# Moving the first weight loads, four kinds of VectorE work and one activation load in a fused linear-attention and mixer kernel

## The chip, the cores and the metric

The kernel runs on one core of a Trainium2 chip. The metric is the device time of one execution in microseconds (us); the median of three runs before the change is 294.98. In the text PE is TensorE, DVE is VectorE, ACT is ScalarE, POOL is GpSimd and SP is SyncE. A "slot" is a place in the kernel's own list of work, explained below.

## What is computed

Inputs are q, k and v (8 batches, 8 heads, 576 positions, head size 64) and the mixer's U, V, w_ch1 and w_ch2. All are 32-bit floats; the kernel works in bf16 with 32-bit sums.

```python
def phi(x, c, s):
    r = np.maximum(x, 0.0)
    return np.concatenate([r * c, r * s], axis=-1)
q_p = phi(q, cos_w, sin_w)
k_p = phi(k, cos_w, sin_w)
kv = np.einsum('bhsf,bhsd->bhfd', k_p, v)
z = np.sum(k_p, axis=2)
num = np.einsum('bhsf,bhfd->bhsd', q_p, kv)
den = np.einsum('bhsf,bhf->bhs', q_p, z)[..., None] + 1e-06
x = num / den                      # heads side by side: (8, 576, 512)
u = x + (x.transpose(0, 2, 1) @ U @ V).transpose(0, 2, 1)
out = u + np.maximum(u @ w_ch1, 0.0) @ w_ch2
```

The weights w_ch1 (512 x 2048) and w_ch2 (2048 x 512) are the same for all batches.

## The kernel before

**Tiles.** A batch's 576 positions are four full tiles of 128 (c = 0 to 3) and a tail of 64 (c = 4); the tails of two batches share a tile. For each batch, `q_prep` and `k_prep` make the features (one cosine and one sine operation for each tile, line 304 on DVE, line 302 on ACT), the q features are transposed (`qtr_unit` on PE for batches 0 and 1, by DMA later), `kv_unit` sums k features times v, and `x_unit` or `x_two` multiply q features by kv and divide by the denominator: a reciprocal on DVE (lines 408 and 409) and the norms, which multiply by it. `x_two` (line 1253) works on a tile in two halves of four heads; its norms are one DVE operation for each half (line 1280), and for batch 1 four ACT operations for each half (line 1274). `A_unit` multiplies by U, its result is cast to `A_sb`, `u_mm` (line 471) multiplies by V, and `u_add` adds x. Then comes the hidden layer, `g1_main` (line 572) with a ReLU on ACT (line 581), and the product with w_ch2: `g2_part` (line 744) for the first two batches, `half_part` (line 873) later. `half_part` multiplies in seven partial products instead of eight; for that it needs sums of hidden tiles (`hid_sum`, line 818) and sums of quarters of w_ch2 in `w2_s[0]` to `w2_s[3]`, made once by `w2_sum` (line 789), each in two halves of 128x1024. It uses them from slot 90 on.

**Order.** The order of work is written out by hand, and every engine runs its instructions strictly in the order in which the program issues them. The start (batch 0, lines 1176 to 1230) is straight code. From there a list `slots` holds the PE work and `todo` what is issued behind each slot: slots 0 to 15 are the hidden layer of batch 0, 16 to 31 products of batch 0, 32 to 47 the hidden layer of batch 1, 48 to 51 the first tails, 52 to 71 further products, 72 to 87 the hidden layer of batch 2, and from 88 on hidden layer and products alternate. `attention_plan` puts the attention of batches 2 to 7 between them: batch 2's `kv_unit` stand at slots 46 and 48, batch 3's at 64 and 66, its `x_two` at 69 and 73. In slot 1 PE comes to the transposes of batch 1's q tail (line 361), behind eight matmuls of `g_half` (line 589) and the four that complete the first two tiles of the hidden layer.

**Transfers.** SP issues the loads of q, k and v in a fixed order; each batch's load is an "odd" and an "even" DMA of 64 rows. One of them waits at SP until the staging buffer (`qst`, `kst`, `vst`) has been read by the features of the batch before, and what is behind it waits too. POOL issues the weights' loads, which cast to bf16 on the way: `load_v0` (heads 0 to 3 of batch 0's v, straight to bf16 in `v0`, an odd and an even half), the four column blocks of w_ch1 (`w1_load`, line 117) and the four blocks of w_ch2 (line 123). POOL also casts U and V (`cast_u`, `cast_v`). Two small copies to `mark` on POOL hold back what follows: the first until batch 0's k has landed (line 1214, ahead of w_ch1), the second until batch 1's k has landed (line 1225, ahead of w_ch2). `gate` (line 1238) is the same on SP: a tiny DMA into `mark2` that must wait for its source. In `first_chain` (line 1113) batch 0 goes from k features to the hidden layer; its last instructions on ACT and DVE are followed directly by batch 1's `q_prep`.

Of the kernel before, what the change touches and what calls it, by code (L numbers as in the profile page):

```python
# [17 lines left out]
def kernel(  # L18
# [11 lines left out]
    nc = tc.nc  # L30
# [12 lines left out]
    TS = 64  # L43
# [13 lines left out]
    class Banks:  # L57
# [21 lines left out]
    qst, kst, vst = [  # L79
        pool.tile([P, H, 5, D], FP32, tag=name, bufs=1, name=name)  # L80
        for name in ("qst", "kst", "vst")
    ]
# [10 lines left out]
    def load_odd(dst, src, b, h0=0, h1=H):  # L93
        nc.sync.dma_start(
            out=dst[1:P:2, h0:h1, 0:4].rearrange("m h c d -> m h (c d)"),
            in_=nines(src, b)[:, h0:h1, 5 * D : 9 * D],
        )
# [17 lines left out]
    def w1_load(n):  # L115
        cs = slice(n * 512, n * 512 + 512)
        nc.gpsimd.dma_start(
            out=w1_bf[:, :, cs], in_=moe_w_ch1.rearrange("(d p) n -> p d n", p=P)[:, :, cs]
        )
# [35 lines left out]
    def load_v0():  # L155
        nc.gpsimd.dma_start(
            out=v0[1:P:2, :, 0:4].rearrange("m h c d -> m h (c d)"),
            in_=nines(v, 0)[:, 0:4, 5 * D : 9 * D],
        )
        nc.gpsimd.dma_start(  # L160
            out=v0[0:P:2].rearrange("m h c d -> m h (c d)"),
            in_=nines(v, 0)[:, 0:4, 0 : 5 * D],
        )
# [92 lines left out]
    def cast_u():  # L256
        cast(G_, U_bf[:, 0:4, :], stU[:, 0:4, :])
        for i in range(2):
            cast(G_, U_bf[tail(i), 4 + i, :], stU[tail(i), 4, :])
# [75 lines left out]
    def kv_unit(b, hg, tag, bufs, eng=None, n=E):  # L335
        if b not in kv_sb:
            kv_sb[b] = pool.tile([P, H, E], BF16, tag="kv", bufs=2, name="kv")
        acc = ps.tile([P, 4, n], FP32, tag=tag, bufs=bufs, name="kv_ps")
        vx = v_ext
        for i in range(4):  # L340
            h = hg * 4 + i
            for c in range(5):
                nc.tensor.matmul(  # L343
                    out=acc[:, i, :],
                    lhsT=k_of(b, c, h),
                    rhs=v_tl[:, h, 0:n] if c == 4 and b < 2
                    else vx[:, c if c < 4 else 4 + b % 2, h, 0:n],
                    start=(c == 0),
                    stop=(c == 4),
                )  # L350
        cast(eng or V_, kv_sb[b][:, hg * 4 : hg * 4 + 4, 0:n], acc)
# [431 lines left out]
    def w2_sum(n, half):  # L783

        a, b = (
            (W2[1], W2[0]), (W2[3], w2_s[0]), (W2[3], W2[1]), (W2[2], w2_s[1])
        )[n]
        js = slice(4 * half, 4 * half + 4)
        V_.tensor_tensor(
            out=w2_s[n][:, js], in0=a[:, js], in1=b[:, js], op=ALU.subtract  # L790
        )
# [171 lines left out]
    def spare(at):  # L963
        if at < 72:
            return ("o", 2) if 32 <= at < 52 else ("g", 3)
        return ("o", 2) if at < 88 else ("s", 1)
# [14 lines left out]
    def attention_plan(b):  # L981

        plan = []
        if b < 4:
            w, f_at, q_eng, k_eng, qtr, lo = PLAN[b]
        else:
            w, q_at, k_at, qtr, lo = PLAN[b]

        def put(at, f, *a, tag=False):
            if tag:  # L990
                a = a + spare(w + at)
            plan.append((w + at, lambda: f(b, *a)))

        for n, c in enumerate(QORD):
            if b > 3:
                put(q_at[0] + q_at[1] * n, q_prep, c, q_at[2:])
                put(k_at[0] + k_at[1] * n, k_prep, c, k_at[2:])
                put(k_at[0] + (3 * n) // 2, v_prep, 0, H, (c,), (G_,))
                continue
            if b == 3:  # L1000
                q_eng, k_eng = V_ if n == 3 else A_, A_ if n < 3 else None
                put((-12, -11, -10, -7, -3)[n], q_prep, c, (q_eng, q_eng))
                put(n - 9 if n < 3 else -5, k_prep, c, (A_, k_eng))
                if n > 2:
                    put(2 * n - 12, k_prep, c, (None, V_))
                put(-4 if n > 2 else -6, v_prep, 0, H, (c,), (A_ if n > 2 else G_,))
                continue
            put(f_at + ((n - 1) % 5 if b == 2 else n), q_prep, c, (q_eng, q_eng))
            put(f_at + 6 + n, k_prep, c, (k_eng, k_eng))
            on_v = b == 2 and n > 2  # L1010
            put(
                -5 if on_v else f_at + 3 + (3 * n) // 2,
                v_prep, 0, H, (c,), (V_ if on_v else G_,),
            )
        for n, (c0, c1) in enumerate(((4, 5), (0, 2), (2, 4))):
            at = qtr[n] if b > 4 else 1 if b == 3 and n == 2 else qtr + 2 * n
            put(at, qtr_dma, c0, c1)
        plan.append((w, lambda: kv_unit(b, 0, *spare(w), A_ if b > 3 else V_)))
        plan.append((w + 2, lambda: kv_unit(b, 1, *spare(w + 2), A_ if b > 3 else V_)))
        for n, c in enumerate(ORD):  # L1020
            if b > 3:
                put(4 + 2 * n, x_unit, c, "X", 1)
            elif n % 2:
                put(9 if (b, n) == (3, 3) else 4 + (3 * n) // 2, x_two, c, tag=True)
            else:
                put(4 + (3 * n) // 2, x_unit, c, "X", 1)
        a_at = 15 - b if b < 4 else 14
        put(a_at, A_unit, tag=True)
        odd = b % 2 == 1


        def two(at):
            return [T1, ("s", 1)] if at >= 88 else [spare(at)] * 2

        plan.append((w + a_at + 2, lambda: u_mm(b, *two(w + a_at + 2))))
        for j in range(4):
            put(a_at + 2 + j + (2 if b > 4 and j > 1 else 0), u_add, j)
        put(a_at + 3, utr_dma, 0, 2)
        put(a_at + (7 if b > 4 else 5), utr_dma, 2, 4)
        if odd:  # L1040
            plan.append(
                (w + a_at + 9, lambda: u_tail(b // 2, *two(w + a_at + 9)))
            )
            put(a_at + 10, utr_dma, 4, 5)
        for at, t in zip(lo, loads(b + 1) if lo else ()):
            plan.append((w + at, t))
        return plan
# [141 lines left out]
    keep_warm(4, "X", 1)  # L1189
    cast_v()  # L1190
    load_v0()
    cast_u()
    spread_v()
    z_all = ps.tile([P, 2, 512], FP32, tag="X", bufs=1, name="z_ps")
# [16 lines left out]
    kv0_mm(kv_lo, range(3, 5))  # L1211
    keep_warm(1, *G3)

    G_.tensor_copy(out=mark, in_=kst[0:TS, 7, 4, 0:1])
    for n in range(4):
        w1_load(n)
    first_chain(0)
    load_odd(qst, q, 1)
    load_even(qst, q, 1)
    load_odd(kst, k, 1)  # L1220
# [32 lines left out]
    def x_two(b, c, *hi):  # L1253
        x_alloc(b)
        rows = slice(0, P) if c < 4 else tail(b)
        if not hi and not side:
            side["g"] = ps.tile([P, 512], FP32, tag="g", bufs=3, name="side")
        lo = ps.tile([P, 512], FP32, tag="T", bufs=1, name="x2_ps")
        up = ps.tile([P, 512], FP32, tag=hi[0], bufs=hi[1], name="x2_ps") if hi else side["g"]
        accs = [  # L1260
            t[:, 0 : 4 * E].rearrange("p (i e) -> p i e", e=E) for t in (lo, up)
        ]
        for h in range(H):
            nc.tensor.matmul(
                out=accs[h // 4][:, h % 4, :], lhsT=qT_of(b, c, h), rhs=kv_sb[b][:, h, :],
                start=(h % 4 == 0), stop=(h % 4 == 3),
            )
        rec = pool.tile([P, 2, 4], FP32, tag="rec", bufs=2, name="rec")
        n = P if c < 4 else TS
        for g, acc in enumerate(accs):  # L1270
            recip(rec[rows, g, :], acc[rows, :, D])
            if b == 1:
                for i in range(4):
                    nc.scalar.activation(
                        out=x_of(b, c)[:, (4 * g + i) * D : (4 * g + i + 1) * D],
                        in_=acc[:, i, 0:D], func=AF.Copy, bias=0.0,
                        scale=rec[:, g, i : i + 1],
                    )
                continue
            nc.vector.tensor_tensor(  # L1280
                out=x_of(b, c, rows)[:, g * 256 : g * 256 + 256].rearrange(
                    "p (i d) -> p i d", d=D
                ),
                in0=acc[rows, :, 0:D],
                in1=rec[rows, g, :].unsqueeze(2).to_broadcast([n, 4, D]),
                op=ALU.mult,
            )
# [18 lines left out]
    def put(at, thunk):  # L1306
        todo.setdefault(at, []).append(thunk)
# [92 lines left out]
    for i, go in enumerate(groups):  # L1400
        slots.append(go)
        if i < 14:
            n, i7 = halfs[i]
# [24 lines left out]
    put(at - 2, lambda: tail_store(nc.sync, 3, o_last(1), slice(0, 512)))  # L1428
    put(at - 1, lambda: tail_store(A_, 2, o_last(0), slice(256, 512)))
    for n in range(8):  # L1430
        put((56, 58, 60, 62, 66, 67, 69, 70)[n], lambda n=n: w2_sum(n // 2, n % 2))
    for j, ts_ in beside.items():
        todo[j] = list(ts_) + todo.get(j, [])

# [49 lines left out]
```

## Time and profile before

| what | value |
|---|---|
| median of 3 runs (lowest, highest) | 294.98 us (294.69, 295.87) |
| the profiled execution | 296.47 us |
| its span, first to last instruction | 294.7 us |
| mean granted TensorE clock | 1.00 |
| share of the chain that ended last | PE 89%, DVE 5%, issue 2%, DMA 2%, ACT 1% |
| HBM read, written | 36.86 MB, 9.44 MB |

How to read the views: a timeline line gives start and length in us, the engine, the line of the kernel, the operation, what it writes and reads, and in brackets how long its engine was idle before it and which engine's work ended that. "x4" means that four alike were merged. "SPq" is SP's queue; a DMA's line there is its issue, not its transfer. The chain of waits follows back from the last instruction what each step waited for. In the DMA view q1 is the queue that SP feeds and q0 the one that POOL feeds; both run on the same 16 DMA engines; its lines give packets, MB, and the packets' own time as a share of the window (over 100% in sum where packets overlap).

### The profile page before, as it was taken

What the parts mean: (1) busy time and instruction counts of PE and PEld (TensorE: products, weight loads), DVE (VectorE), ACT (ScalarE), POOL (GpSimd) and SP (SyncE); (2) the same over time, 40 slices, a digit from 0 to 9 for tenths busy, and PEclk for the clock granted to TensorE, in tenths of its full rate; (3) what the DMA queues carried; (4) which work ended last, traced back from release to release, by engine and by line L of the source; (5) the groups of instructions that cost most, each with busy time, mean ns of one, the idle gap of its engine ahead of it and who ended that gap; (6) DMA issues with size and microseconds to landing.
All of it is one profiled execution on the core that took longest, in us unless ns stands there. A gap on an engine that the chain in (4) does not pass through costs nothing.

```text
span 294.7 us, 7180 instructions
## 1 busy us (share of the span) xinstructions
PE 285.6 (97%) x2884; PEld 194.3 (66%) x2922; DVE 210.1 (71%) x503; ACT 157.6 (53%) x305; POOL 50.5 (17%) x89
## 2 busy tenths in 40 slices
PE   8999999999989999999999999999999999999995
PEld 6685554446645445676757666766877668889884
DVE  4988745694698978837736794678747788785863
ACT  2956853175890357568735865378752334446310
POOL 8800400012020001310500311031200100000340
PEclk9999999999999999999999999999999999999999
DMA  6999999999996999999499919992900141101013
GB/s 215 337 252 254 255 195 186 204 317 252 325 145 92 300 260 243 225 304 308 122 231 283 266 38 242 237 342 56 221 31 2 73 89 73 72 2 71 2 72 145
DMA packets 90709, 54.07 MB, mean 183 GB/s; under 512 B 58420, under 2 KB 87380, under 8 KB 90676
## 3 DMA queue, kind: packets, MB, share of 16 engines
q1 hardware_dynamic: 84116, 43.85, 59.7%
q0 software_dynamic: 6416, 9.63, 14.6%
q8 instruction: 23, 0.38, 0.5%
q10 hardware_dynamic: 144, 0.13, 0.1%
q14 instruction: 10, 0.08, 0.1%
HBM read 36.86 MB, written 9.44 MB: 157 GB/s over the span
## 4 chain that ended last, share of the span: by engine, by line
PE 89%; DVE 5%; issue 2%; DMA 2%; ACT 1%; DVEq 0%; ACTq 0%
PE g_ps L572 32%; PE h_ps L873 26%; PE o_ps L744 8%; PE gt_ps L706 5%; PE c_ps L666 4%; PE kv_ps L343 3%; PE x_ps L418 3%; DMA qst<-in_q_dram 2%; PE h_ps L744 1%; PE a_ps L441 1%; DVE k_p L304 1%; PE t_ps L373 1%; PE va_ps L471 1%; PE t_ps L361 1%; DVE x_bf L428 1%
## 5 line engine op out<-in xcount | busy, mean ns | idle before, releaser
L581 ACT ACTIVATE hid<-g_ps 128x512 bf16<-128x512 f32 x112 | 66.6, 597 | 85.0 <-PE g_ps L572 84.7
L572 PE MATMUL g_ps<-uT,w_bf 128*128 128x512 bf16 x414 | 105.1, 379 | 1.3
L572 PEld LDWEIGHTS <-w_bf 128*128 128x128 bf16 x440 | 41.4, 98 | 36.8
L873 PEld LDWEIGHTS <-hid 128*128 128x128 bf16 x480 | 45.4, 98 | 9.6
L873 PE MATMUL h_ps<-w_bf,hid 128*128 128x256 bf16 x288 | 37.0, 273 | 0.0
L831 DVE TENSOR_TENSOR o_sb<-u_bf,h_ps 128x256 f32<-128x256 bf16 x44 | 18.3, 416 | 18.2 <-PE h_ps L873 17.9
L744 PE MATMUL o_ps<-w_bf,hid 128*128 128x512 bf16 x122 | 29.4, 379 | 0.4 <-issue 0.2
L131 POOL CAST v_ext<-vst 128x512 bf16<-128x512 f32 (+1 forms) x26 | 17.9, 716 | 52.2 <-DMA vst<-in_v_dram 42.5
L873 PE MATMUL h_ps<-w_s,S 128*128 128x256 bf16 x208 | 26.5, 273 | 0.0
L873 PE MATMUL h_ps<-w_s,hid 128*128 128x256 bf16 x192 | 24.9, 272 | 0.0
L931 POOL DMA_DIRECT2D out_dram<-o_sb x16 | 10.0, 625 | 85.5 <-DVE o_sb L831 84.0
L831 DVE TENSOR_TENSOR o_sb<-o_sb,h_ps 128x256 f32<-128x256 f32 (+1 forms) x36 | 15.5, 432 | 11.1 <-PE h_ps L873 10.7
L873 PEld LDWEIGHTS <-S 128*128 128x128 bf16 x208 | 20.0, 98 | 4.3
L479 DVE TENSOR_TENSOR u_bf<-x_bf,va_ps 128x512 bf16<-128x512 bf16 x27 | 17.8, 679 | 6.5 <-PE va_ps L471 4.2
L744 PEld LDWEIGHTS <-hid 128*128 128x128 bf16 x128 | 11.6, 98 | 12.5
L706 PE MATMUL gt_ps<-uT_tl,w_bf 128*128 128x128 bf16 x256 | 16.1, 219 | 0.0
L428 DVE TENSOR_TENSOR x_bf<-x_ps,rec 128x512 bf16<-128x512 f32 x22 | 15.2, 691 | 0.8
L706 PEld LDWEIGHTS <-w_bf 128*128 128x128 bf16 x256 | 15.0, 98 | 1.0
L302 ACT ACTIVATE k_p<-kst,cosw 128x512 bf16<-128x512 f32 x20 | 14.2, 713 | 0.1
L302 ACT ACTIVATE q_p<-qst,sinw 128x512 bf16<-128x512 f32 x18 | 12.6, 709 | 2.5 <-DMA qst<-in_q_dram 2.5
L604 DVE TENSOR_TENSOR hid<-kept,c_ps 128x256 bf16<-128x256 f32 x24 | 9.4, 418 | 5.6 <-PE c_ps L666 2.8
L408 DVE TENSOR_SCALAR rec<-x_ps 128x8 f32<-128x8 f32 (+2 forms) x39 | 6.3, 161 | 8.5 <-PE x_ps L418 7.5
(186 smaller groups left out, 422.0 us busy)
## 6 DMA issues: line engine op xcount, KB each, us to landing
qst<-in_q_dram SPq DMA_DIRECT2D x14, 512.0 KB, 5.7
kst<-in_k_dram SPq DMA_DIRECT2D x14, 512.0 KB, 6.8
vst<-in_v_dram SPq DMA_DIRECT2D x12, 512.0 KB, 6.8
out_dram<-o_sb POOLq DMA_DIRECT2D x19, 256.0 KB, 3.5
w_bf<-in_moe_w_ch_dram POOLq DMA_DIRECT2D x8, 512.0 KB, 13.4
out_dram<-o_sb SPq DMA_DIRECT2D x16, 256.0 KB, 2.8
qst<-in_q_dram SPq DMA_DIRECT2D x2, 640.0 KB, 8.9
kst<-in_k_dram SPq DMA_DIRECT2D x2, 640.0 KB, 8.1
```

The lines of the kernel that those rows point to most:

```text
L131: eng.tensor_copy(out=o, in_=i)
L302: nc.scalar.activation(out=o, in_=i, func=AF.Relu, bias=0.0, scale=w)
L428: nc.vector.tensor_tensor(out=x_of(b, c, rows).rearrange("p (g i d) -> p g i d", g=2, d=D), in0=view[:, :, :, 0:D], in1=rec[rows].unsqueez ...
L479: nc.vector.tensor_tensor(out=u_bf[b][:, j, :, :], in0=x_bf[b][:, :, ns], in1=va[b][j].rearrange("p (c n) -> p c n", c=4), op=ALU.add,)
L572: nc.tensor.matmul(out=g_ps.rearrange("p (c t) -> p c t", c=4), lhsT=w1_bf[:, d, j * P : j * P + P], rhs=uT[b][:, d, :, :], start=(d == 0) ...
L581: nc.scalar.activation(out=hid[b][:, j, :], in_=g_ps, func=AF.Relu, bias=0.0, scale=1.0)
L666: nc.tensor.matmul(out=w[to].rearrange("p (c t) -> p c t", c=2), lhsT=lhs[:, d, cs], rhs=rhs[:, d], start=(first and d == 0), stop=(d == 1 ...
L706: nc.tensor.matmul(out=g_ps[:, jj, :], lhsT=w1_bf[:, d, j * P : j * P + P], rhs=uT_tl[pr][:, d, :], start=(d == 0), stop=(d == 3),)
L744: nc.tensor.matmul(out=o[:, cols], lhsT=lhs[:, j, c * P : c * P + P], rhs=w2_bf[:, j, cols], start=(j == 0), stop=(j == NJ - 1),)
L831: eng.tensor_tensor(out=o, in0=x, in1=y, op=ALU.add)
L873: nc.tensor.matmul(out=acc, lhsT=lhs[:, j, :], rhs=rhs[:, j, :], start=(j == 0 and at is not None), stop=(j == 7), skip_group_check=at is ...
L931: eng.dma_start(out=out[b].rearrange("(m k) n -> m k n", k=9)[:, c : c + 6 : 5, :], in_=halves[b, n]["o"][i],)
```

## The change

Five edits. (1) The first two column blocks of w_ch1 are issued on POOL right behind `load_v0`, ahead of `cast_u`, with nothing that holds them back; the last two stay where they were, but the copy to `mark` ahead of them now reads `k_tl`, so that they wait for the cosine features of batch 0's k tail instead of k's landing. (2) On SP a tiny DMA that reads a `v0` element of an odd row is put ahead of the loads of batch 1's q, so that these, and all that is behind them on SP, wait for the odd half of `load_v0`. (3) The eight `w2_sum` go from slots 56 to 70 to slots 44 to 50 (the first four) and 82 to 87 (the last four). (4) Batch 3's norms in `x_two` go from DVE to ACT. (5) The casts of batch 3's two `kv_unit` go from DVE to ACT.

```diff
-        plan.append((w, lambda: kv_unit(b, 0, *spare(w), A_ if b > 3 else V_)))
-        plan.append((w + 2, lambda: kv_unit(b, 1, *spare(w + 2), A_ if b > 3 else V_)))
+        plan.append((w, lambda: kv_unit(b, 0, *spare(w), A_ if b > 2 else V_)))
+        plan.append((w + 2, lambda: kv_unit(b, 1, *spare(w + 2), A_ if b > 2 else V_)))
...
     load_v0()
+    for n in range(2):
+        w1_load(n)
     cast_u()
...
-    G_.tensor_copy(out=mark, in_=kst[0:TS, 7, 4, 0:1])
-    for n in range(4):
+    G_.tensor_copy(out=mark, in_=k_tl[0:TS, 7, 0:1])
+    for n in range(2, 4):
         w1_load(n)
     first_chain(0)
+    nc.sync.dma_start(out=mark2, in_=v0[1:2, 0, 0, 0:1])
     load_odd(qst, q, 1)
...
-            if b == 1:
+            if b in (1, 3):
                 for i in range(4):
                     nc.scalar.activation(
...
-        put((56, 58, 60, 62, 66, 67, 69, 70)[n], lambda n=n: w2_sum(n // 2, n % 2))
+        put((44, 45, 49, 50, 82, 84, 85, 87)[n], lambda n=n: w2_sum(n // 2, n % 2))
```

## The prediction

> **What bounds the kernel now.** I read the page first, then the chain of waits, then the timelines of two stretches and the DMA view of three.
>
> ```profile
> span 294.7 us, 7180 instructions
> PE 285.6 (97%) x2884; PEld 194.3 (66%) x2922; DVE 210.1 (71%) x503; ACT 157.6 (53%) x305; POOL 50.5 (17%) x89
> ```
>
> TensorE (PE) is busy for 97% of the span, so a gain has to come from one of the few places where PE waits. The change works at two: the start, and the stretch around 86 us. The chain of waits from 10 to 32 us (start, length, what) shows the first:
>
> ```profile
> 12.36 0.69 DVE k_p L304
> 13.05 0.71 issue
> 13.77 1.62 DVE k_p L304 x3
> 15.38 0.05 issue
> 15.43 0.35 PE z_ps L1201 x8
> ...
> 23.09 1.67 PE g_ps L589 x7
> 24.77 0.86 PE g_ps L572 x4
> 25.63 0.45 PE t_ps L361 x8
> ```
>
> Until 15.4 the end is set by VectorE (DVE) making batch 0's k features. From 15.4 on PE follows without a pause: 23.09 is the first matmul of the hidden layer, 25.63 the transposes of batch 1's q. The two views of line 304 (min/median/max ns), before and after 14.4 us, show that the features are slow only at first:
>
> ```profile
> L304 DVE TENSOR_SCALAR k_p<-kst,cosw x3: 745/816/823, 12.4 to 13.8; 128x512 bf16<-128x512 f32 x3
> ```
> ```profile
> L304 DVE TENSOR_SCALAR k_tl<-kst,cosw x1: 474/474/474, 15.3 to 15.3; 128x512 bf16<-128x512 f32 x1
> ```
>
> The same operation takes 0.8 us, then 0.47. In the timeline the four w_ch1 issues stand on GpSimd (POOL) exactly there, and batch 1's q is first used at 23.5:
>
> ```profile
> 11.36 2.98 POOL L117 DMA_DIRECT2D w_bf<-in_moe_w_ch_dram  x4
> ```
> ```profile
> 23.50 0.71 ACT L302 ACTIVATE q_tl<-qst,sinw 128x512 bf16<-128x512 f32 x1
> ```
>
> **Part 1a: w_ch1's issues leave k's features.** The six DVE features start 0.67, 0.74 and 0.74 us apart while POOL issues, 0.40 apart afterwards. Without the issues three steps shorten from 2.15 to 1.19: **0.96 us**. The first two issues now follow v0's on POOL, about 9.14 to 10.65 (0.75 each), beside two DVE features of q (9.31 and 9.74) and the start of q's evacuations. If each feature is held until its issue ends, as k's were, the evacuations start some 0.6 later. DVE waits 0.34 for PE before q_tlT at 11.75, which absorbs about half. I give back 0.3; bounds 0 (v0's issues at 7.52 and 8.31 left q's features at 0.47 to 0.51) and 0.6. Gain 0.65, bounds 0.3 and 0.96. POOL's casts of U move from 9.14 to 10.65; U is first used at 20.2, so that costs nothing. The last two issues wait for k_tl's cosine half (about 14.9 now) and then stand beside v_ext's cast (0.55 us at 15.69, wanted by PE at 17.7): hidden.
>
> **Part 1b: q of batch 1 waits for v0.** Before, its two loads were issued at 9.90 and 10.61 and landed at 19.54, 4 us ahead of their first use. SP now waits for v0's first half (issue 7.52, 5.9 us to land: 13.4), issues the gate's small transfer, and then the loads: 0.87 lies between a gate and the next issue at 38.78, so 14.3, and 0.7 later 15.0. k's loads are queued behind them, but these waited for k's features until 15.44 anyway. What q meets is the point. Queue q1 is SP's, q0 POOL's; three windows of the DMA view, 13.3 to 15.4, 20 to 30 and 39.7 to 43.3:
>
> ```profile
> q1 hardware_dynamic: 641, 0.72, 96.1%
> q0 software_dynamic: 23, 0.01, 4.3%
> ```
> ```profile
> q0 software_dynamic: 1178, 1.17, 69.1%
> q1 hardware_dynamic: 1179, 1.31, 45.9%
> ```
> ```profile
> q0 software_dynamic: 747, 0.74, 124.4%
> ```
>
> In the first, q's transfer has the engines to itself: 641 packets in 2.1 us, 305 per us, because w_ch1's packets only begin at 15.5, 4.1 us after their issue. In the second, k beside w_ch1, the queues share one to one: 118 packets per us each. In the third SP has issued u_bf at 39.65 and not one of its packets has run by 43.3, while POOL's queue flows: a start takes at least 3.65 us then. With the change w_ch1 flows from about 13.2 (9.14 + 4.1), so q's 1024 packets (64 rows by 8 heads, twice) meet the second and third case. Start 14.3 + 3.7 = 18.0; 1024/118 = 8.7 more: 26.7; half a us to land: **27.2**. Bounds: as long as before, 8.9 from the second issue: 23.9; as long as k's pair (first issue 15.44, POOL's wait for it ends at 30.1, so 14.6): 28.9. I take 27.2, since k's pair is the nearest row and it also had the tail of q ahead of it. The Trainium skill, "DMA: Bandwidth & Descriptors", Specifications, gives about 0.6 us to the first byte for SP's kind of queue; by it q would land at 14.3 + 0.6 + 8.7 + 0.5 = 24.1 and the whole sum would be -1.0, 294.0, as in the first rival below. The third window above disagrees with it for a start beside a loaded queue.
>
> Behind q: ScalarE (ACT) runs in order, q_tl's sine stands ahead of all the hidden layer's ReLUs, and PE after twelve matmuls stands at the transposes of q_tl. Landing to ACT's start is 0.11 (7.56 to 7.67), the sine 0.71, to PE 0.05: transposes at 27.2 + 0.87 = 28.07 instead of 25.47. **+2.6 us**, in which 1a's gain has disappeared: q must land by 24.6 for no loss, by 23.95 for the gain of 0.65. After it PE has 0.215 us per matmul to do without pause to 42 us, and nothing there waits for a clock time: k lands later, about 31.5, but is wanted later too; v lands earlier, since w_ch1 is done by 28. So nothing is given back.
>
> **Part 2: w2_sum and batch 3.** PE's timeline and DVE's:
>
> ```profile
> 86.76 0.41 PE L471 MATMUL va_ps<-A_sb,V_bf 32*128 32x128 bf16 x16 [0.76 <-DVE A_sb L131]
> ```
> ```profile
> 81.24 1.08 DVE L789 TENSOR_TENSOR w_s<-w_bf 128x1024 bf16<-128x1024 bf16 x1
> ...
> 84.42 1.08 DVE L789 TENSOR_TENSOR w_s<-w_bf 128x1024 bf16<-128x1024 bf16 x1
> ...
> 86.42 0.28 DVE L131 CAST A_sb<-a_ps 128x128 bf16<-128x128 f32 x1
> ```
>
> PE idles 0.76 for the cast of A_sb, whose input was ready at 84.1; two sums of 1.08 stand ahead of it. Both go, so the cast comes about 2 us earlier: **-0.76**. The next late thing would be x_bf at 83.36, in time for PE at 83.70. The first four sums go to slots 44 to 50, 66 to 75 us: DVE there idles 2.08, 1.93 and 1.62 before 70.57, 72.94 and 74.98; 4 x 0.68 fits, cost 0 (0.3 if one hits the next x_unit). Batch 3's norms (four of 0.42) and kv casts go to ACT, which idles 11.03 us before 98.85; the second tile's eight operations, 0.2 apart, fall among ReLUs at 101, each with three banks of lead: 0, bounds -0.2 and +0.4. The last four sums go to slots 82 to 87. There DVE has a backlog and one pause:
>
> ```profile
> 114.60 0.69 DVE L818 TENSOR_TENSOR S<-hid 128x1024 bf16<-128x1024 bf16 x1 [1.24 <-ACT hid L581]
> ```
>
> 2.7 us added against 1.24 free makes S and what follows 1.5 late. S is wanted by PE at 118.9 and ready at 116.0 now, so it holds; four steps on, the X bank is read out at 121.39 and wanted at 122.54: 0.35 short. **+0.3**, bounds 0 and 1.5.
>
> **Sum.** 2.6 - 0.76 + 0.3 = +2.1 us. On the profiled execution, 296.47 (span 294.7 and 1.8 around it), 298.6; that execution is 1.49 above the median of 294.98, so on the median **297.1**.
>
> **Rivals.**
> 1. *q still in time.* The loads take as long as before and land at 23.9: -0.65 - 0.76 + 0.3 = -1.1, **293.9** (293.3 with the full 0.96 and no cost in part 2). For it: w_ch1's first two pieces, 1024 packets, could have run by 18.6, with the next two issued only at 15 and 4.1 us from flowing. Against: that gap is at most half a us. It decides from a landing before 24.6 on; before 23.95 nothing of the gain is lost. Chance 0.22.
> 2. *q a little late*, 24 to 26: q starts 1.4 us after its issue, as the kernel's first load did, and shares: 14.3 + 1.4 + 8.7 + 0.5 = 24.9: +0.3 - 0.46: **294.8**. Chance 0.15.
> 3. *Slower still: the clock falls.* PE would stand still from 24.8 to 28.1, 3.3 us; the longest pause of the profile is 0.76 and the granted clock 1.00 throughout, so no row shows what follows. If it costs half the rate for as long as the pause, +1.65: **298.8**. Which length of pause is enough no row shows, only that 0.76 is not. The Trainium skill, "TensorE: Matmul & The Clock Gate", What's actually happening, says that an idle window of about 3.4 us halves the clock; by that rule this case begins just past my forecast. Chance 0.07.
> 4. *The gate isn't what it says*: if it waits for all of v0 (14.26), q lands 0.85 later, within the forecast's range.
>
> **Numbers.** Forecast (q at 26 to 28.9) 0.56: 297.1, its own range 295.9 to 298.8. The range from 293.6 to 298.8 takes in rivals 1 and 2 but for 293.3. A difference under 0.5%, 1.5 us, can't be told from none here. Over 296.45: most of the forecast and the third rival, 0.52; within: 0.36; below 293.5: part of the first rival, 0.12.
>
> **What would show it.** Line 304 at 0.47 us throughout k's features and z_ps before 15; q landing after 25, and ACT's q_tl waiting on it with PE's longest idle time ahead of line 361; no idle time at A_sb. I am wrong if w_ch1's packets still start at 15.5, or if q1 gets more than half of the engines.

## The result, and the profile after

The changed kernel takes 300.04 us (median of 21 runs, 296.0 to 302.8). The kernel before, run beside it on the same chip, takes 296.58 (21 runs, 294.69 to 299.24). The ratio is 1.0094, with a 95% interval from 1.0068 to 1.012: slower by about 0.9%, 2.8 us. The slowest runs, over 1.5% above the fastest of their kernel (three of the changed kernel, 301.42 to 302.8), are left out of that ratio, so it isn't the quotient of the medians, which stand 3.5 us apart. The forecast was +0.7%, at 297.1, in a range up to 298.8: the sign is right, the time is above the range.

The profiled execution of after took 300.31 us, its span is 298.5 and its mean granted clock 0.994. Its page begins:

```profile
span 298.5 us, 7236 instructions
PE 289.1 (97%) x2922; PEld 194.9 (65%) x2922; DVE 206.2 (69%) x497; ACT 161.7 (54%) x323; POOL 50.8 (17%) x89
```

PE has 3.5 us more of busy time than before. Part of that is matmuls that run slower, as will be seen, and 38 more matmul records are in this trace. The chain of waits from 10 to 29 us (start, length, what):

```profile
12.47 1.45 DVE k_p L304 x4
...
13.97 0.48 DVE k_p L304
14.51 0.35 PE z_ps L1203 x8
...
15.70 12.41 DMA qst<-in_q_dram
...
28.20 0.73 ACT q_tl L302
28.97 0.74 PE t_ps L361 x8
```

k's features go through at 0.47 us each (four in 1.45 us of chain, where three took 1.62 before), and the fourth group of z_ps matmuls comes at 14.51 instead of 15.43. But from 15.70 on the chain is one transfer, batch 1's q, for 12.41 us. ACT's q_tl waits for it, and PE's transposes of line 361 wait for ACT. PE's timeline of that stretch, with the idle time in brackets:

```profile
22.00 1.90 PE L589 MATMUL g_ps<-uT,w_bf 128*128 128x512 bf16 x8
23.74 1.03 PE L572 MATMUL g_ps<-uT,w_bf 128*128 128x512 bf16 x4
28.97 0.74 PE L361 MATMUL t_ps<-ident,q_tl 128*128 128x128 bf16 x8 [4.21 <-ACT q_tl L302]
```

The first hidden matmul comes at 22.00, 1.09 earlier than before (0.32 of it because batch 0's q landed sooner: its first feature on DVE starts at 7.37, before at 7.69), and the transposes at 28.97, 3.50 later: between the two 4.59 us are lost, 4.21 of them as plain idle time. Then PE is slow as well: two g_ps matmuls of line 572 take 1.06 us at 29.51 and 0.59 at 33.72. The table by windows (start and end, length, busy time of each engine) says why; the third column from the end is the clock granted to PE:

```profile
28.50:29.00 0.50, 0.03 (x1) 0.03 (x2) 0.50 (x3) 0.50 (x2) 0.00 (x0) 1.00 1.06 383
29.00:30.00 1.00, 1.00 (x10) 0.72 (x11) 1.00 (x4) 0.89 (x2) 0.00 (x0) 0.67 1.07 389
30.00:31.00 1.00, 1.00 (x8) 0.73 (x7) 1.00 (x3) 0.40 (x1) 0.00 (x0) 0.50 1.08 391
...
32.50:33.00 0.50, 0.50 (x3) 0.24 (x2) 0.50 (x2) 0.41 (x1) 0.50 (x1) 0.76 0.65 207
33.00:33.50 0.50, 0.50 (x7) 0.33 (x6) 0.01 (x1) 0.03 (x1) 0.50 (x2) 1.00 0.29 99
```

From 29.33, just after PE has started again, its clock is halved for 3.41 us, which costs 1.7. The third group of transposes of line 361 comes at 33.43 instead of 28.25 (+5.18: 3.50 and 1.68). Later PE gets a little back. The idle time at A_sb has gone:

```profile
91.11 0.40 PE L471 MATMUL va_ps<-A_sb,V_bf 32*128 32x128 bf16 x16
```

The lag behind before is 5.19 us at the matmuls of a_ps (83.70 before, 88.89 after), 4.35 at this line (86.76 before), and 3.8 at the end. So the whole difference of the two spans is -1.09 (start) + 4.59 (q) + 1.68 (clock) - 0.84 (A_sb) - 0.55 (several small waits behind it) = 3.8 = 298.5 - 294.7.

The granted clock averaged over a run tells whether it met such a stretch: 3.41 us at half rate in 298.5 is a mean of 0.9943. Of after's 21 runs five have a mean of 0.998 or more; they took 296.0 to 297.62, with a median of 297.1. The other 16 lie between 0.989 and 0.994 and took 298.49 to 302.8. So some three runs in four meet such a stretch (where, only the profiled one shows). Of before's 81 runs in the three later comparisons nine have a mean of 0.994 or less.

### The profile page after: what moved, and what is told of

The parts are those of the page before. It is cut to its first block, busy times and chain, and to the rows that moved or that the text cites. A ratio compares the mean times of both kernels' runs of the same rounds, so it can differ in the third digit from the quotient of the medians.

```text
span 298.5 us, 7236 instructions
## 1 busy us (share of the span) xinstructions
PE 289.1 (97%) x2922; PEld 194.9 (65%) x2922; DVE 206.2 (69%) x497; ACT 161.7 (54%) x323; POOL 50.8 (17%) x89
## 3 DMA queue, kind: packets, MB, share of 16 engines
q0 software_dynamic: 6416, 9.63, 14.3%
## 4 chain that ended last, share of the span: by engine, by line
PE 88%; DMA 6%; DVE 4%; issue 1%; ACT 0%; DVEq 0%; ACTq 0%
PE g_ps L572 32%; PE h_ps L873 26%; PE o_ps L744 10%; DMA qst<-in_q_dram 6%; PE gt_ps L706 5%; PE c_ps L666 4%; PE kv_ps L343 3%; PE x_ps L418 3%; PE h_ps L744 1%; PE t_ps L361 1%; PE a_ps L441 1%; DVE q_p L304 1%; PE va_ps L471 1%; DVE k_p L304 1%; PE va_ps L492 0%
## 5 line engine op out<-in xcount | busy, mean ns | idle before, releaser
L572 PE MATMUL g_ps<-uT,w_bf 128*128 128x512 bf16 x440 | 108.3, 382 | 0.0
L744 PE MATMUL o_ps<-w_bf,hid 128*128 128x512 bf16 x128 | 30.1, 379 | 0.0
L831 DVE TENSOR_TENSOR o_sb<-o_sb,h_ps 128x256 f32<-128x256 f32 (+1 forms) x36 | 15.4, 430 | 10.1 <-PE h_ps L873 9.9
L744 PEld LDWEIGHTS <-hid 128*128 128x128 bf16 x128 | 11.6, 98 | 12.5
```

What stands on the lines that cost most here:

```text
L572: nc.tensor.matmul(out=g_ps.rearrange("p (c t) -> p c t", c=4), lhsT=w1_bf[:, d, j * P : j * P + P], rhs=uT[b][:, d, :, :], start=(d == 0) ...
L744: nc.tensor.matmul(out=o[:, cols], lhsT=lhs[:, j, c * P : c * P + P], rhs=w2_bf[:, j, cols], start=(j == 0), stop=(j == NJ - 1),)
L831: eng.tensor_tensor(out=o, in0=x, in1=y, op=ALU.add)
```

## The experiments

Theory A: the late landing of q is all of the loss, made by hold and early w_ch1 together: the hold issues q 5 us later, w_ch1 halves its rate. The clock falls when PE's pause is long enough. Rivals: B, the hold alone makes q late, w_ch1 has no part in it; C, the early w_ch1 pair alone does it; D, part 2's moved sums or norms cost something. All ratios are to the kernel before on the same chip, with 95% intervals. Each "one look" number is from that kernel's profiled execution.

**The hold taken out of after.**

```diff
-    nc.sync.dma_start(out=mark2, in_=v0[1:2, 0, 0, 0:1])
```

> The changed kernel without the wait of batch 1's q for v0; the early w_ch1 pair, the sums, norms and casts stay moved. Theory (the hold makes q land at 28.1, TensorE idles 4.2 us for it and its clock then falls): q is issued at 9.9 and 10.6 again, shares the DMA engines with w_ch1 from about 12.7 and lands before 23; no idle time ahead of line 361, granted clock 1.00, first hidden matmul still at 22.0; in all about -1.1 at the start and -0.8 to -1.4 later: ratio 0.992 to 0.994 of before. Rival (w_ch1's early start alone makes q late, held or not): q lands after 25, TensorE idles 1 to 2 us ahead of line 361: ratio 0.997 to 1.002.

0.9979 [0.9955, 1.0004], 295.47 us. q is issued at 10.25, lands at 25.17, and PE waits 0.99 us for it, as the rival had it. No run of 12 shows a clock under 1.0. So the hold is the larger part of the loss, and without it nothing is lost that the runs can tell. But q, issued 0.35 later than in before, lands 5.6 later (19.54 before): the early pair alone moves it this far. From 16 to 24 us this kernel's DMA view has both queues at one rate:

```profile
q0 software_dynamic: 944, 0.94, 69.4%
q1 hardware_dynamic: 946, 1.07, 46.3%
```

**The hold alone in before.**

```diff
+    nc.sync.dma_start(out=mark2, in_=v0[1:2, 0, 0, 0:1])
     load_odd(qst, q, 1)
```

> The kernel before with the wait of q for v0 alone. Theory: q is issued at 14.9 and 15.6 just as w_ch1 begins to flow at 15.5, so it shares and lands at 25 to 28; TensorE idles 1 to 3.5 us ahead of line 361; the clock may or may not fall: ratio 1.004 to 1.014. Rival (only the early w_ch1 pair makes q late; without it the wait is harmless): q lands before 23.7, no idle time there: ratio 1.000.

1.0174 [1.0118, 1.023], 302.45 us: more than was expected, and at least as slow as the whole change. In the profiled execution (303.52 us, one of the longer of six), with four w_ch1 pieces issued at 11.6 to 14.3, all ahead of q (14.69), q lands at 29.68 and PE waits 6.24. The clock is halved for two lengths of 3.41, 27.77 to 34.60, as the table by windows shows (columns as above; PE's count in its bracket):

```profile
27.50:28.00 0.50, 0.00 (x0) 0.00 (x0) 0.00 (x0) 0.00 (x0) 0.00 (x0) 0.77 1.16 265
28.00:31.00 3.00, 0.36 (x4) 0.46 (x5) 1.29 (x4) 1.23 (x3) 0.00 (x0) 0.50 1.08 374
31.00:34.00 3.00, 3.00 (x19) 1.91 (x17) 2.71 (x6) 1.06 (x2) 0.25 (x2) 0.50 1.08 389
```

Here w_ch1 is issued in its old place. So the loss doesn't need the early pair, and theory A is wrong in that point: the hold is enough where w_ch1's queue flows beside q.

**The early pair alone in before** (first edit of the change, no hold, nothing of part 2).

```diff
     load_v0()
+    for n in range(2):
+        w1_load(n)
...
-    G_.tensor_copy(out=mark, in_=kst[0:TS, 7, 4, 0:1])
-    for n in range(4):
+    G_.tensor_copy(out=mark, in_=k_tl[0:TS, 7, 0:1])
+    for n in range(2, 4):
```

> The kernel before with w_ch1's early pair alone, q not held. Theory: k's features at 0.47 us each, first hidden matmul 1.0 to 1.1 us earlier, q in time: ratio 0.996 to 0.997. Rival (w_ch1's early start makes q late): idle time ahead of line 361 eats it: ratio 0.999 to 1.004.

1.002 [0.9993, 1.0047], 296.53 us: no difference, as the rival had it, but not for its reason. q, issued at 9.49, lands at 24.77, and PE doesn't pause at line 361. In the profiled execution (298.69 us, 2.2 above the median) it loses 2.2 us further on, for batch 1's k, which lands at 34.79: ACT's feature of its tail waits for it, a ReLU stands behind that feature, and PE waits for the ReLU (timeline of ACT and PE; the last w_ch1 piece had landed just before, at 34.62):

```profile
34.88 0.72 ACT L302 ACTIVATE k_tl<-kst,sinw 128x512 bf16<-128x512 f32 x1 [3.20 <-DMA kst<-in_k_dram]
36.14 2.12 PE L572 MATMUL g_ps<-uT,w_bf 128*128 128x512 bf16 x8 [2.06 <-ACT hid L581]
```

The pair's gain at k's features isn't seen at the first hidden matmul either, which comes at 23.12 (23.09 before): the even half of `load_v0`, which PE also needs, lands at 15.79 here and at 14.26 before.

**Part 2 alone in before** (edits 3, 4 and 5), and **the moved sums alone** (edit 3).

```diff
-        put((56, 58, 60, 62, 66, 67, 69, 70)[n], lambda n=n: w2_sum(n // 2, n % 2))
+        put((44, 45, 49, 50, 82, 84, 85, 87)[n], lambda n=n: w2_sum(n // 2, n % 2))
```

and, in part 2 alone, also

```diff
-        plan.append((w, lambda: kv_unit(b, 0, *spare(w), A_ if b > 3 else V_)))
+        plan.append((w, lambda: kv_unit(b, 0, *spare(w), A_ if b > 2 else V_)))
...
-            if b == 1:
+            if b in (1, 3):
```

> The kernel before with the moved sums and batch 3's norms and casts alone. Theory (from the changed kernel's trace: the idle time of 0.76 ahead of line 471 is gone, and about 0.5 more between there and the end): -0.8 to -1.4 us: ratio 0.995 to 0.997. Rival, as predicted: 0.3 of the 0.76 is given back by the sums in slots 82 to 87: -0.5: ratio 0.998 to 0.999.

> The kernel before with w2_sum's new places alone. Theory (the sums held A_sb's cast at 86 us): the idle time of 0.76 ahead of line 471 is gone: -0.7 to -1.0 us: ratio 0.9965 to 0.998. Rival (it takes the norms' move as well): idle time stays over 0.4 there, ratio 0.999 to 1.000.

0.9975 [0.9949, 1.0] and 0.9982 [0.9967, 0.9997], 295.06 and 295.34 us. Both lose the idle time at A_sb, so D falls: part 2 costs nothing. Its gain, about 0.2% as forecast, is at the edge of what the runs can tell. Nothing in either trace waits for the sums at slots 82 to 87. The norms and casts of batch 3 weren't tried by themselves. In part 2's trace one wait is new, and it is not DVE's (PE's timeline):

```profile
159.84 0.43 PE L418 MATMUL x_ps<-kv,q_pT 128*128 128x65 bf16 x8 [2.11 <-DMA q_pT<-q_p]
```

Batch 5's q is transposed by DMAs on SP's queue, and in this execution they came later than PE. Before has no such wait in its trace. PE isn't early here (its matmuls of a_ps come at 83.41 us, in before's second look at 82.44 and without such a wait), so why the transposes were late is open.

**w_ch1's last pair held until q has landed.** After, with the copy to mark and the last two pieces behind q's loads:

```diff
-    G_.tensor_copy(out=mark, in_=k_tl[0:TS, 7, 0:1])
-    for n in range(2, 4):
-        w1_load(n)
...
+    G_.tensor_copy(out=mark, in_=qst[0:TS, 7, 4, 0:1])
+    for n in range(2, 4):
+        w1_load(n)
```

> The changed kernel, hold included, with w_ch1's last pair issued only when batch 1's q has landed. Theory (q's packets start at 17.5 and its second load then shares one to one with w_ch1's last pair from 19 on): with nothing to share with, q lands at 21 to 22, in time for 23; no idle time there; the last w_ch1 pieces land at about 29 and 33, just in time or up to 1 us late: ratio 0.991 to 0.996. Rival (the late issue alone is what makes q late): q lands after 25 all the same: ratio 1.003 to 1.010.

0.9981 [0.9952, 1.001], 295.37 us. q is held as in after and issued at 14.01, and yet lands at 22.60: 8.6 us from issue, where after needs 13.2. From 18.8 to 21.8 its queue has the engines to itself:

```profile
DMA packets 1014, 1.15 MB, mean 383 GB/s; under 512 B 32, under 2 KB 1013, under 8 KB 1013
...
q1 hardware_dynamic: 1008, 1.13, 104.9%
```

So B falls too: a hold to 14 us costs nothing if nothing shares with q afterwards. What shares with q in after is mainly this last pair, issued at 15.30 and 16.04; the early pair had landed by 20.25. What is left over in this kernel is 0.94 us lost near 31 for w_ch1's third piece, issued 7.5 us later.

**More or fewer early pieces, no hold.** After without the gate, as in the first experiment, and with one of w_ch1's four pieces early and three behind k's features; then with none early:

```diff
-    for n in range(2):
-        w1_load(n)
+    w1_load(0)
...
-    for n in range(2, 4):
+    for n in range(1, 4):
```
```diff
-    for n in range(2):
-        w1_load(n)
...
-    for n in range(2, 4):
+    for n in range(4):
```

> The changed kernel without the hold and with one w_ch1 piece early instead of two, the other three behind k's features. Theory (without the hold q still landed at 25.2 since 1024 packets of w_ch1 stood beside it from 12.7 on; with 512 it shares half as long): q lands at 21 to 23, no idle time ahead of line 361, the second piece is needed at about 25.5 and lands by 24.5: first transposes at 24.5 instead of 25.5: ratio 0.992 to 0.995. Rival (w_ch1 flows on without a break, since the second piece is issued at 15.4 and the queue still has the first): q at 25 as before: ratio 0.997 to 0.999.

> The changed kernel without the hold and with all four w_ch1 pieces behind k's features. Theory (w_ch1's packets start 3.5 to 4 us after their issue): k's features at 0.47, q alone on the engines and landed by 19, but w_ch1 starts at 18.5 to 19 beside k of batch 1 and its first piece lands at 22.5 to 24.5 against a use at 22: TensorE waits 0.5 to 2.5 us ahead of line 589: ratio 0.996 to 1.003. Rival (the first piece, ahead of k in its queue, lands by 22): no wait: ratio 0.992 to 0.994.

One early: 0.9971 [0.9942, 0.9999], 295.88 us, q lands at 24.28, not at the 21 to 23 expected. None early: 1.0058 [1.0019, 1.0096], q lands at 18.46, and PE waits 1.81 us at 22.4 for w_ch1's own first piece, as the theory had it, though the ratio is above its range. With two early it was 25.17. The step in q's landing lies between none and one: w_ch1's queue has only to flow while q's packets run. Two of the twelve runs of the kernel with none early took over 700 us; why isn't known.

**PE kept busy through the pause.** After, with filler matmuls (16, then 8, into an unused bank) ahead of the transposes that wait for q, which compute nothing that is used:

```diff
+        if n == 0:
+            at(1, lambda: keep_warm(16, "X", 1))
```

> The changed kernel with 16 extra matmuls of zeros (16 x 0.215 = 3.4 us, their result unused) in slot 1, ahead of the transposes for which TensorE stood still. Theory (a late q costs 3.5 us of waiting, and the clock's fall another 1.7 that a busy TensorE would not pay): q lands at 28 as before, the idle time ahead of line 361 shrinks to under 1 us, the granted clock stays 1.00 from 28 to 33 us, and the time falls by about 1.7 us below that of the changed kernel: ratio 1.003 to 1.005 of before. Rival (the fallen clock is a mark of these runs and not a cost of the pause, or q lands later still): ratio 1.008 to 1.011.

> The changed kernel with 8 extra matmuls of zeros (1.72 us, result unused) in slot 1 instead of 16. Theory (the pause costs twice: its length and a fall of the clock): TensorE is busy to 26.3 and then waits under 2.5 us, the clock stays up and nothing is added to the wait, so the time is 1.0 to 1.8 us under that of the changed kernel in the same call, and not above that of the version with 16. Rival (16 measured no gain since the clock costs nothing): the same time as the changed kernel, within 0.5 us.

1.0095 [1.0067, 1.0123] and 1.0076 [1.0045, 1.0106], 299.1 and 298.33 us. With 16 no run of six fell below a mean clock of 0.998, and the transposes came at 28.03. The ratio missed its expectation of 1.003 to 1.005 all the same, and lies in the rival's 1.008 to 1.011. The fillers took 0.5 us of it (q landed at 26.67, so that the transposes could have come at 27.54), and PE, which was 2.6 us ahead of after at A_sb, then idled 1.44 at 162 for batch 5's q.

With 8, four of twelve runs still have a mean of 0.994; they took 299.21 to 300.91, the other eight 296.84 to 299.11. So q's lateness costs time with no fall of the clock at all, and the fall comes on top; how much is the pause's own varies: the runs with no fall stand 0.5 us above before in after's comparison, 1.6 and 2.2 in the repeat below, 1.8 with 8 fillers, 3.3 with 16 (with the fillers' own cost in the last two). Nor are all falls shown to come from this pause: with 8 fillers it is 0.85 us in the profiled execution, which has no fall, and no trace shows where the four runs with a fall have theirs.

**After and before again**, nothing changed.

> The changed kernel again, for a second profile and for runs on the same chip as the version with 8 extra matmuls. Theory: q lands at 26.5 to 28.5, TensorE idles 3 to 4.5 us ahead of line 361; runs with a granted clock of 0.995 or less are 1.5 to 3 us longer than those at 1.00: ratio 1.006 to 1.012. Rival (the first profile was an outlier): q lands before 25, idle time under 1.5.

> The kernel before again, for a second profile. Theory (how much w_ch1's issues slow k's features is a matter of the phase between two engines, since two other runs with the same issues showed 0.61 to 0.63 in two or three features only): between 0.3 and 1.0 us lost in the six features; q lands at 19 to 21; idle time of 0.5 to 0.9 ahead of line 471 at 86. Rival (0.96 lost, as in the first profile, is the rule): three features at 0.74 or more.

After: 1.0128 [1.0074, 1.0181], 300.73 us. Two of its six runs have a clock of 1.0 and took 297.87 and 298.51; the other four took 300.51 to 302.18. The profiled one had a pause without a fall:

```profile
28.59 0.61 PE L361 MATMUL t_ps<-ident,q_tl 128*128 128x128 bf16 x8 [3.34 <-ACT q_tl L302]
```
```profile
25.20:28.50 3.30, 0.05 (x1) 0.00 (x0) 0.81 (x3) 0.75 (x2) 0.00 (x0) 1.00 1.16 252
28.50:30.00 1.50, 1.41 (x19) 1.24 (x20) 1.50 (x5) 1.27 (x3) 0.00 (x0) 1.00 1.08 372
```

Before, one look: 294.4 us, with two of the costs that the change takes away smaller than in the execution that the prediction was made from. Its k features alternate between 0.47 and 0.61 us instead of standing at 0.8, and PE doesn't idle at A_sb, where 0.5 to 0.9 was expected:

```profile
84.67 0.40 PE L471 MATMUL va_ps<-A_sb,V_bf 32*128 32x128 bf16 x16
```

With the hold alone PE idles 0.51 there, with the early pair alone not at all. So of the four traces with the sums in their old place two show that wait; none of the ten with the sums moved does.

No kernel tried beats before by more than the 0.5% that can be told. The lowest ratio, 0.9971 with one early piece, isn't told apart from the others, and the median of its twelve runs, 295.88, is no lower than before's beside it, 295.77.

## Why the prediction was right in sign and wrong in size

**The step that failed: rival 3, the clock.** The prediction gave the fall a chance of 0.07 and said that it begins "just past my forecast". Its price was right, +1.65 against 1.7 measured in the profiled execution; its chance was not: about three runs in four meet such a fall. Without it that execution's sum is 3.8 - 1.7 = 2.1, the forecast's figure, and that is in part luck: q cost 0.9 more than forecast (the transposes come 3.50 later, against 2.6), and A_sb with what is behind it gave 0.9 more back (-0.84 - 0.55 against -0.76 + 0.3). Two things were wrong in the chance. The time that PE loses ahead of line 361 was forecast at 3.3 us and is 4.59 (4.21 as the profile counts idle time), because it grows at both ends: PE got there 1.09 earlier, not 0.65, and q 0.9 later. And a threshold on the length of a single pause isn't what the traces show. In after the low stretch begins at 29.33, 0.36 us after PE had started again, and the 3.41 us before it (25.92 to 29.33) hold those 0.36 us of work; with the hold alone it begins 3.4 us after PE's last matmul and lasts two lengths without a break, although PE is back at 30.64, in the first. Both fit stretches of 3.41 us, one after the other, that are judged as a whole and not counted from the pause's start. In the repeat of after the edges of these stretches lie at 23.82, 27.23 and 30.64 (worked out from the first change of its clock, at 6.75, in steps of 3.413). They split the pause of 3.34, which runs from 25.25 to 28.59: PE is busy for 1.43 us in the first stretch and for 2.04 in the second, and the clock stays. If so, a pause of about that length brings the fall or not by where it lies, and one chance in fourteen was far too low. The Trainium skill, "TensorE: Matmul & The Clock Gate", What's actually happening, says that the window is 3413 ns and "free-running"; the traces of after, of its repeat and of the hold alone agree. I took the window's length from that section and left out that it has its own phase.

**The level.** The forecast stood on a median of three runs, 294.98. The same kernel's 21 runs in the comparison have 296.58. The forecast of +2.1 put on that is 298.7. This moved the time by 1.6 us against a range that was made of causes within the kernel only. Each of the two misses alone would have left the time within the range (297.1 + 1.6 = 298.7, 297.1 + 1.7 = 298.8); together they passed its end.

**1b, q held: right in place and mechanism, 0.9 short.** Forecast: issue 14.3, landing 27.2, transposes at 28.07. Measured: 14.95, 28.11 and 28.97. The first 0.65 are the gate, since v0's odd half landed at 14.04 and not 13.4, with w_ch1 behind it. The sharing, 1024 packets at 118 per us, is as forecast; the DMA view of after from 20 to 27 us, 116 per us each:

```profile
q0 software_dynamic: 817, 0.82, 68.9%
q1 hardware_dynamic: 815, 0.94, 46.3%
```

The start after 3.7 us was too late by a little: q's packets begin at 17.5, 2.6 us after the issue, and have the engines nearly to themselves from 18 to 19. (The 3.65 had been read off a DMA transpose, and q is a plain load.) The lot comes out 0.25 later all the same. By the 0.6 us to the first byte (the Trainium skill, "DMA: Bandwidth & Descriptors", Specifications), which the prediction weighed, an estimate of the landing from the same issue is 24.7; the trace disagrees, with 2.6 us to the first packet and 28.11.

**1a, k's features: right in the profiled execution, not shown beyond it.** The gain is 0.92 us at z_ps and 1.09 at the first hidden matmul, against 0.65; without the 0.32 by which batch 0's q landed sooner it is 0.60 and 0.77. The 0.3 that I gave back were needed: beside the early issues q's last two features on DVE take 0.73 and 0.82 us, before 0.51 and 0.47 (DVE's timeline of after):

```profile
9.21 0.73 DVE L304 TENSOR_SCALAR q_p<-qst,sinw 128x512 bf16<-128x512 f32 x1
9.87 0.82 DVE L304 TENSOR_SCALAR q_tl<-qst,cosw 128x512 bf16<-128x512 f32 x1
```

Counted from q's first feature, k's features start 0.35 later than before (5.02 us against 4.67). But the price of 0.96 for the old place belongs to one execution. From the first to the last start of DVE's six features it is 2.93 us in before and 1.98 in after, but 2.23 in before's second look, 2.25 with the hold alone and 2.26 with part 2 alone, all with the four issues in their old place; with the sums alone it is 2.98 again. So the issues cost 0.25 to 1.0 there, it seems by how they fall between the features, and the upper end was taken for the kernel's price. At the first hidden matmul no gain stands out from the spread between executions: it comes at 21.83 to 23.64 in the five traces with all issues in their old place, and at 21.60 to 23.12 in the seven with the pair early.

**"Nothing is given back" was almost right.** k's odd half landed at 30.13 and its even half by 31.89, when POOL's copy that waits for it starts (forecast: about 31.5), and PE didn't wait for them. From A_sb to the end 0.55 us came back in small waits. What the prediction did not look for is that batch 5's transposed q can come late (2.11 us in part 2 alone, 1.44 with 16 fillers); no run shows why.

**Part 2: -0.76 and +0.3.** A_sb's wait went, -0.84 by the lag. The +0.3 at slots 82 to 87 was not found: PE shows no wait ahead of the sums' users in after, and the sums alone are at 0.9982. Part 2 is worth about -0.2% in the runs, half to three quarters of a us; two of four traces with the sums in their old place have no wait at A_sb at all, so here too one execution overstated it.

**Rival 1 and rival 2** fall: q at 28.1 lies past 24.6, from which the first decides, and past the second's 26. Rival 2's landing, 24 to 26, is that of the change without its hold (25.17). Rival 4: the gate was issued 0.01 after v0's odd half had landed (14.04) and well ahead of the even half (14.94), so it is what it says.

What stays open: whether the place of the pause decides in the other runs of after too, or q's landing does, since only two of its executions have a trace; and why the runs without a fall stand 0.5 us above before in the first comparison, where the sum without a fall was +2.1.

## What to carry to other kernels

A load that is held back for another's sake keeps its deadline: add up issue, start and its share of the engines behind whatever flows by then, and compare that with its first use before asking what the hold gains. Here q, issued at 14 us, was in time with the engines to itself; issued at 15 beside a second queue, it cost PE 4.6 us. A pause of TensorE near 3.4 us has to be priced with the low clock that may follow, as a chance and not as a threshold. And a duration or an idle time of under 1 us from one execution is a sample: a second trace of the same kernel cut one cost to a quarter and had nothing of another.

## What the runs showed of the hardware

**A flowing POOL queue costs more than its half.** Beside w_ch1 q's queue moves 118 packets per us, and both together 251 GB/s; with the engines to itself (18.8 to 21.8 us, w_ch1's last pair held) it moves 1008 packets in 3.0 us, 336 per us, at 383 GB/s. So q's rate falls to a third, not to a half. In after, POOL's queue by itself (15.4 to 17.4) moved 206 GB/s.

**The clock is halved in steps of 3.41 us.** One step after a pause of 4.21, two without a break around one of 6.24, none after one of 3.34. In all fourteen traces each change of the clock comes a whole number of 3.413 us after the first one (7 steps to the fall in after and with the hold alone, 3 with one early piece), and the first one comes anywhere from 3.88 to 7.20 us. What makes a step count as idle stays open. In the step ahead of a fall PE was busy for 0.36 us in after and for 0.05 with the hold alone; but with one early piece a fall came at 15.71 behind a step with 41 matmuls and 2.86 us of busy time, where PE hadn't idled over 0.52 us at once. The step at the same place in before (41 matmuls, 2.96 us) brought none, nor did one with 1.43 us in the repeat of after.
